# Splitting the expert weights once and keeping the halves in DRAM, in a fused filter, maxout and expert kernel

## The chip, the cores and the metric

One core of a Trainium2 chip runs the whole program. The metric is the device time of one execution in microseconds (us); three executions of the kernel before were timed. The trace is one profiled execution on that core.

## The reference, cut to what matters

Eight batches of 3072 tokens with 256 channels are filtered in the frequency domain, passed through a maxout layer and a projection, and then each token goes to one of eight experts.

```python
y = irfft(rfft(x, axis=1) * F)                      # 24576 tokens x 256
x = max(y @ w1, y @ w2, y @ w3) @ w_out             # 256 -> 768 -> 256
expert_idx = argmax(normalized(x) @ normalized(emb).T / tau)
for e in range(8):
    h = maximum(x[mask] @ w1[e], 0)                 # 256 -> 1024
    out[mask] = gate_w[mask, None] * (h @ w2[e])    # 1024 -> 256
```

With the reference's own data the experts get 6555, 2627, 10962, 295, 744, 233, 3084 and 76 tokens.

## The kernel before, in words

Every product that matters is made from operands in two parts: the high part is the operand rounded to the short type of TensorE's fast float32 (float32r), the low part is what is left, and a product is three matmuls (high by high, high by low, low by high). `split` (L189) makes the two parts of a tile: ScalarE copies the tile into the high part (L190) and VectorE subtracts (L191).

The program is written out by hand in one order (`manual_schedule`); a main loop `for x in range(18 * 49)` (L1129) walks through points. A unit `u` of 18 points carries 512 tokens through the maxout: at each point TensorE does six matmuls of 512 columns (`f_group`, L481), at points 3 to 6 the projection of the unit before (`x2_tile`, L510), at 6, 7, 11 and 12 the transform back of the unit after (`g_mm`, L451), whose data `g_load` (L431) fetches from the DRAM tensor `s2` on SyncE's queue at point 0 into tiles `gt`; `g_split` splits them at points 3 and 8. `x2_store` (L588) writes a unit's rows to the DRAM tensor `x2d`, from which tokens are gathered later. From unit 38 on (`RELEASE`, L42) the spectral stages are over and their SBUF is free.

Then the tokens go through the experts in slots: a slot is 256 tokens of one expert, and there are exactly 100 here (26, 11, 43, 2, 3, 1, 13 and 1 for the eight experts, from the counts above). The slots are listed expert by expert; `tables` (L870) turns counts into that list, for the first 12 slots early and for the other 88 at the end of the routing. `slots` (L1064) issues a slot in four steps j:

- `up(s, j)` (L1025): 12 matmuls of 256 columns, a quarter of w1 by the slot's tokens; the sum `psh` becomes `h` in two parts (ScalarE L1035, VectorE L1036).
- `down(s - 1, 0)` and `down(s - 1, 1)` (L1040) at j = 1 and 2: 24 matmuls each of the slot before by its w2; ScalarE scales the sum into `o` (L1052), and `o_store` (L1054) scatters it with two indirect DMAs from GpSimd.
- `x_load` (L985) gathers the tokens of slot s + 3 (two indirect DMAs from GpSimd), `x_turn` (L998) transposes them by DMA from SyncE's queue into `xw`, and `x_split` (L1003) joins and splits them into `xT`.
- `w_load(s + 3)` (L974): two indirect DMAs from GpSimd gather 1 MB of w1 and 1 MB of w2 of the slot's expert, as float32, into one of two buffers `raws`. Where the slot two before had the same expert, the row numbers are out of bounds and nothing is moved (L935, L940 to L944).
- `w_part(s + 1, j)` (L1014): at every j a quarter of the next slot's weights is split, whether it was loaded anew or not, into one of two buffers `ws`: one of its own (`w0`, in the trace `w`) and the memory of the maxout weights (`wt`).

So per slot TensorE has 96 matmuls of 256 columns, ScalarE and VectorE have four splits of 128 x 1024 beside their other work, and GpSimd has six indirect DMAs. The tiles `o`, `xw` and `xf` share a pool `g` of three buffers.

Of the kernel before, what the change touches and what calls it, by code (L numbers as in the profile page):

```python
# [10 lines left out]
F32 = mybir.dt.float32  # L11
F32R = mybir.dt.float32r
# [29 lines left out]
RELEASE = 18 * 38  # L42


# [66 lines left out]

def _bits(w):
    w = np.ascontiguousarray(w)
    return w.view(np.int64) if w.dtype == np.float64 else w


def _layout(inputs):
# [17 lines left out]
    c32[:, 26:26 + 128] = np.arange(128)  # L135
    return {
# [21 lines left out]
def fft_filter_maxout_moe_kernel(ctx: ExitStack, tc: tile.TileContext, I, out):  # L158
# [13 lines left out]
    lst = nc.dram_tensor("lst", (LROWS + 1, SLOT), I32, kind="Internal").ap()  # L172
    lst1 = lst.rearrange("r (c o) -> (r c) o", o=1)
# [9 lines left out]
    pidx, sgn, iotas = c32[:, 24:25], c32[:, 25:26], c32[:, 26:26 + 128]  # L183
    base_fin = const.tile([128, E], F32, name="base_fin")
# [8 lines left out]
    def body():  # L193
        st = ExitStack()
        with st:
# [231 lines left out]
            # ------------------------------------------------ back to tokens, channel major  # L427
# [48 lines left out]
            # ------------------------------------------------ maxout, projection, routing  # L476
# [33 lines left out]
            def x2_tile(u, t):  # L510
# [15 lines left out]
                def evac():  # L526
                    # lower and upper halves of the words apart, for the transposes of the slots
# [29 lines left out]
            def route2(u):  # L557
                """Steps from the norms to the one-hot choice and the gate."""
# [36 lines left out]
            def route3(u):  # L595
                """Steps from the choice to the places in the experts' lists."""
# [46 lines left out]
            # ------------------------------------------------ setup  # L643
# [21 lines left out]
            def w_split(key, n, hi, lo, late=False):  # L665
# [4 lines left out]
                # a float64 is (1 + h * 2^-20 + l * 2^-52) times a signed power of two: the high  # L670
                # part takes the first 12 bits, the low part the value of all the others
# [77 lines left out]
            class Decode:  # L749
                """Loads and decodings in order, a load ahead of the decodings, at most so many of these at a time."""  # L750
# [93 lines left out]
            def due(x):  # L844
                """Work wanted by point x: the least steep way to keep every deadline."""
# [24 lines left out]
            def tables(at, n, upto, rnd):  # L870
                """Steps to the expert and the list row of slots at .. at + n, from the counts upto."""
                tag = f"_{at}"
                cnt, ni, nf, se, ss = t8("cnt" + tag), t8("ni" + tag, dt=I32), t8("nf" + tag), t8("se" + tag), t8("ss" + tag)
# [16 lines left out]
                # list row of the slot numbered by the partition  # L890
# [8 lines left out]
                dve.tensor_scalar(out=sm, in0=pidx, scalar1=lastv, scalar2=None, op0=ALU.min)  # L899
# [164 lines left out]
            def slots(first, end):  # L1064
                """Points of the expert slots first .. end, of which lead() has made two ready."""
                for s in range(first, end + 1):
                    on, near = s < end, first < s < end - 1
                    for j in range(4):
# [9 lines left out]
                        if near:  # L1078
                            w_part(s + 1, j)
# [149 lines left out]
```

## Time and profile before

| | |
|---|---|
| median of three runs | 3392.07 us (3390.06 to 3402.77) |
| span of the profiled execution | 3398.8 us (it has no other time of its own) |
| TensorE busy | 3210.7 us, 94% |
| VectorE, ScalarE, GpSimd busy | 2499.9, 2068.2, 1541.9 us |
| DMA, mean over the span | 100 GB/s |
| first product of the slots | at 2126.8 us |
| last matmul | at 3388.1 us |

The span is the time from the first to the last instruction of the profiled execution, 6.7 us above the median of the timed runs. A TensorE that counts as busy need not run at its peak: a matmul's own time covers its way through the array, and the next begins well before it ends. How fast a row of matmuls really goes is read from the distance of their starts.

### The profile page before, as it was taken

The numbers are of one execution on the slowest core, as the hardware profiler recorded it, in microseconds if no ns is written. First come the engines' busy times: TensorE is split into PE (matmuls) and PEld (weight loads), VectorE is DVE, ScalarE is ACT, GpSimd is POOL, SyncE is SP. The second block draws the span as 40 slices with busy tenths as digits, with TensorE's granted clock in tenths as the row PEclk, the third lists the DMA queues.
The fourth block names the chain that finished last, engine by engine and source line by source line (L and its number), as shares of the span: only waits on it lengthen the run. The fifth ranks groups of instructions, "written<-read, shape, count | busy, mean of one in ns | idle before, by whom it ended". The sixth has DMA issues, their size and how long they took to land. (4 is left out here: it accounts for less than half of the span.)

```text
span 3398.8 us, 57541 instructions
## 1 busy us (share of the span) xinstructions
PE 3210.7 (94%) x20524; PEld 2860.8 (84%) x20524; DVE 2499.9 (74%) x4617; ACT 2068.2 (61%) x3818; POOL 1541.9 (45%) x1294
## 2 busy tenths in 40 slices
PE   5899999989999999999999999899999999999998
PEld 2678888878788888888888888899999999999898
DVE  7678687776788656878545555788888888888786
ACT  3444545546555554455444344788888888888786
POOL 3233233232333212333222232677777777777674
PEclk6899999999999999999999999999999999999999
DMA  8756456466554433453100120322334222224622
GB/s 247 223 135 135 126 136 142 125 120 164 122 117 112 101 122 84 98 104 94 49 26 32 32 86 23 61 65 65 107 72 113 63 65 66 66 65 127 167 65 66
DMA packets 313606, 338.58 MB, mean 100 GB/s; under 512 B 164248, under 2 KB 233251, under 8 KB 309604
## 3 DMA queue, kind: packets, MB, share of 16 engines
q1 hardware_dynamic: 217012, 197.53, 26.0%
q0 software_dynamic: 55088, 86.98, 9.5%
q10 hardware_dynamic: 41216, 50.35, 4.6%
q8 instruction: 164, 2.69, 0.4%
q14 instruction: 126, 1.03, 0.1%
HBM read 387.18 MB, written 107.42 MB: 146 GB/s over the span
## 5 line engine op out<-in xcount | busy, mean ns | idle before, releaser
L187 PE MATMUL p<-y,wt 128*128 128x512 f32 x5184 | 1327.0, 400 | 4.9 <-DVE m L498 2.9
L187 PEld LDWEIGHTS p<-y,wt 128*128 128x128 f32 x5184 | 956.9, 190 | 210.9 <-DVE m L498 3.3
L187 PEld LDWEIGHTS pso<-wo,h 128*128 128x128 f32 x3456 | 447.3, 188 | 17.5 <-DVE h L228 0.2
L187 PE MATMUL pso<-wo,h 128*128 128x264 f32 x3456 | 453.1, 285 | 0.0
L354 POOL TENSOR_TENSOR t<-t,ft 96x256 f32<-96x256 f32 (+1 forms) x176 | 178.4, 1014 | 586.7 <-DVE t L350 287.3
L191 DVE TENSOR_TENSOR wt<-r,wt 128x1024 fp32r<-128x1024 f32 x200 | 340.4, 1702 | 77.2 <-issue 53.1
L191 DVE TENSOR_TENSOR w<-r,w 128x1024 fp32r<-128x1024 f32 x200 | 336.7, 1684 | 71.9 <-issue 51.2
L1057 POOL DMA_INDIRECT out<-o,ti x200 | 286.4, 1432 | 220.0 <-ACT o L1052 186.9
L472 POOL TENSOR_TENSOR y<-df,sm 128x256 fp32r<-128x256 f32 x192 | 152.5, 795 | 501.4 <-DVE df L471 500.4
L625 POOL DMA_INDIRECT lst<-ids,pi x192 | 214.8, 1119 | 332.3 <-DVE gs L228 146.3
L187 PE MATMUL psh<-xT,wt 128*128 128x256 f32 x2400 | 322.2, 284 | 44.6 <-DVE wt L191 41.5
L977 POOL DMA_INDIRECT r<-in_e,wi x200 | 332.1, 1661 | 61.7 <-issue 31.7
L187 PE MATMUL psh<-xT,w 128*128 128x256 f32 x2400 | 325.5, 285 | 29.2 <-DVE w L191 27.4
L187 PEld LDWEIGHTS psh<-xT,wt 128*128 128x128 f32 x2400 | 297.2, 190 | 55.8 <-DVE wt L191 51.8
L190 ACT ACTIVATE wt<-r 128x1024 fp32r<-128x1024 f32 x200 | 335.9, 1680 | 0.0
L187 PEld LDWEIGHTS psh<-xT,w 128*128 128x128 f32 x2400 | 301.5, 191 | 39.6 <-DVE w L191 36.7
L190 ACT ACTIVATE w<-r 128x1024 fp32r<-128x1024 f32 x200 | 325.8, 1630 | 0.0
L227 ACT ACTIVATE h<-m 128x512 fp32r<-128x512 f32 x288 | 181.4, 630 | 236.5 <-DVE m L502 227.6
L989 POOL DMA_INDIRECT xg<-x2d,ti x200 | 285.7, 1428 | 61.9 <-issue 61.6
L187 PE MATMUL pso<-w,h 128*128 128x256 f32 x2400 | 305.6, 284 | 0.0
L187 PE MATMUL pso<-wt,h 128*128 128x256 f32 x2400 | 299.5, 280 | 4.0 <-DVE h L1036 3.4
L187 PEld LDWEIGHTS pso<-w,h 128*128 128x128 f32 x2400 | 296.3, 193 | 0.0
(159 smaller groups left out, 4809.7 us busy)
## 6 DMA issues: line engine op xcount, KB each, us to landing
ft<-in_filt SPq DMA_DIRECT2D x160, 192.0 KB
x2d<-r SPq DMA_DIRECT2D x48, 514.0 KB
xt<-in_x SPq DMA_DIRECT2D x96, 256.0 KB
s<-ot ACTq DMA_DIRECT2D x96, 256.0 KB
gt<-s SPq DMA_DIRECT2D x94, 256.0 KB
bt<-bmd SPq DMA_DIRECT2D x160, 144.0 KB
zt<-s SPq DMA_DIRECT2D x80, 192.0 KB
s<-ot ACTq DMA_DIRECT2D x80, 192.0 KB
```

Source lines behind the costliest of these rows:

```text
L187: pe.matmul(out=o, lhsT=l, rhs=r, start=start, stop=stop)
L190: act.activation(out=hi, in_=src, func=ACTF.Copy)
L191: (eng or dve).tensor_tensor(out=lo, in0=src, in1=hi.bitcast(F32), op=ALU.subtract)
L227: act.activation(out=hi, in_=src, func=ACTF.Copy)
L354: later(1, lambda: pool.tensor_tensor(out=t, in0=t, in1=fb, op=ALU.mult))
L472: later(1, lambda: pool.tensor_tensor(out=yl, in0=df, in1=sm, op=ALU.add))
L625: s = pool.indirect_dma_start(out=lst1, out_offset=bass.IndirectOffsetOnAxis(ap=pi[:, t:t + 1], axis=0), in_=ids[:, t:t + 1], in_offset=No ...
L977: pool.indirect_dma_start(out=t, out_offset=None, in_=src, in_offset=off, bounds_check=E * 128 - 1, oob_is_err=False)
L989: pool.indirect_dma_start(out=g[:, t], out_offset=None, in_=x2d[0:n], in_offset=bass.IndirectOffsetOnAxis(ap=slot[s][:, t], axis=0), bound ...
L1057: d = pool.indirect_dma_start(out=out, out_offset=bass.IndirectOffsetOnAxis(ap=slot[s][:, t], axis=0), in_=o[:, t], in_offset=None, bounds ...
```

## The change

The weights of all experts are split once, into two DRAM tensors `wsd` (16.8 MB each; a row holds the high and then the low part). `presplit` does this between units 38 and 45: 32 pieces of 128 x 1024, one every four points, each loaded on SyncE's queue (512 KB), split by ScalarE and VectorE into a tile `wsp`, and stored on SyncE's queue (1 MB). The slots then gather the two parts directly, w1 and w2 as one indirect DMA each of 2 MB (128 rows of 16 KB), into three buffers instead of two; `w_part`, `raws` and the splits in the slots are gone. A slot keeps the weights of the slot three before it, and the slot list is dealt out as three runs that take turns (`_runs`): slots 0, 3, 6, ... walk through the first third of the list, 1, 4, 7, ... through the second, and so on. The tile `o` moves from pool `g` to pool `m1`.

```diff
+NW = 3
+W_READY = RELEASE + 4 * 32 + 14
+def _runs(n):
+    at = np.arange(128)
+    size = (n + NW - 1 - np.arange(NW)) // NW
+    start = np.cumsum(size) - size
+    return np.where(at < n, start[at % NW] + at // NW, at)
...
+    wsd = [nc.dram_tensor(f"wsd_{i}", (E * 128, 4096), F32, kind="Internal").ap() for i in range(2)]
...
-                dve.tensor_scalar(out=sm, in0=pidx, scalar1=lastv, scalar2=None, op0=ALU.min)
+                dve.tensor_scalar(out=sm, in0=turn, scalar1=lastv, scalar2=None, op0=ALU.min)
...
-                    dve.tensor_tensor(out=sf, in0=es, in1=cols["es"][:, at - 2:at + n - 2], op=ALU.is_equal)
+                    dve.tensor_tensor(out=sf, in0=es, in1=cols["es"][:, at - NW:at + n - NW], op=ALU.is_equal)
...
-            def w_load(s):
-                off = bass.IndirectOffsetOnAxis(ap=cols["wi"][:, s:s + 1], axis=0)
-                for t, src in zip(raws[s % 2], (e1, e2)):
-                    pool.indirect_dma_start(
-                        out=t, out_offset=None, in_=src, in_offset=off, bounds_check=E * 128 - 1, oob_is_err=False
-                    )
+            def w_load(s, i):
+                pool.indirect_dma_start(
+                    out=ws[s % NW][i].bitcast(F32), out_offset=None, in_=wsd[i],
+                    in_offset=bass.IndirectOffsetOnAxis(ap=cols["wi"][:, s:s + 1], axis=0),
+                    bounds_check=E * 128 - 1, oob_is_err=False,
+                )
+            def presplit():
+                def load(i):
+                    e, j = divmod(i, 4)
+                    raw = raw_p.tile([128, 1024], F32, tag="raw", name="raw")
+                    src = (e1, e2)[j // 2][128 * e:128 * e + 128, 1024 * (j % 2):1024 * (j % 2) + 1024]
+                    sp.dma_start(out=raw, in_=src)
+                    return raw
+                def put(i, t):
+                    e, j = divmod(i, 4)
+                    dst = wsd[j // 2][128 * e:128 * e + 128].rearrange("p (a q) -> p a q", a=2)
+                    sp.dma_start(out=dst[:, :, 1024 * (j % 2):1024 * (j % 2) + 1024], in_=t.bitcast(F32))
+                nxt, last = load(0), None
+                for i in range(4 * E):
+                    raw, nxt = nxt, load(i + 1) if i + 1 < 4 * E else None
+                    yield
+                    t = sp_p.tile([128, 2, 1024], F32R, tag="sp", name="wsp")
+                    src = raw.rearrange("p (m c) -> p c m", c=8) if i % 4 < 2 else raw
+                    hi, lo = (t[:, a].rearrange("p (c m) -> p c m", c=8) if i % 4 < 2 else t[:, a] for a in range(2))
+                    act.activation(out=hi, in_=src, func=ACTF.Copy)
+                    yield
+                    dve.tensor_tensor(out=lo, in0=src, in1=hi.bitcast(F32), op=ALU.subtract)
+                    yield
+                    if last is not None:
+                        put(i - 1, last)
+                    last = t
+                    yield
+                put(4 * E - 1, last)
...
-                        g_p.tile([128, 2, D], F32, tag="g", name="o"),
+                        m1_p.tile([128, 2, D], F32, tag="m1", name="o"),
...
+                    if s == first:
+                        w_load(s + 2, 0)
...
-                        if near:
-                            w_part(s + 1, j)
                         if j == 2:
...
-                        if j == 3 and first < s < end - 3:
-                            w_load(s + 3)
+                            if s + 2 < end:
+                                w_load(s + 2, 1)
+                        if j == 3 and s + 3 < end:
+                            w_load(s + 3, 0)
```

A yield of `presplit` is one point. `w_first(0)` (at `W_READY`, unit 45, point 16) gathers the weights of slots 0 and 1; the third buffer is the memory of the maxout weights again, so slot 2's gather is issued at the start of slot 0.

**The order on VectorE, one slot.** Ahead of the change (`r` raw weights, `w` and `wt` the two buffers of split weights, `psh` the up product, `h` its low part, `gate`, `xf`, `xT` gates and tokens of the next slot):

```order
L191 TENSOR_TENSOR wt<-r_1_20840,wt 128x1024
L1036 SCALAR_TENSOR_TENSOR h_27694<-psh,h_27694 128x512
L1006 COPY gate<-xg 128x4
L1010 COPY xf<-xw 128x2x2x128
L191 TENSOR_TENSOR xT<-xf,xT 128x512
L191 TENSOR_TENSOR wt<-r_1_20840,wt 128x1024
L1036 SCALAR_TENSOR_TENSOR h_27747<-psh,h_27747 128x512
L191 TENSOR_TENSOR wt<-r_1_20841,wt 128x1024
L1036 SCALAR_TENSOR_TENSOR h_27806<-psh,h_27806 128x512
L191 TENSOR_TENSOR wt<-r_1_20841,wt 128x1024
L1036 SCALAR_TENSOR_TENSOR h_27830<-psh,h_27830 128x512
```

With the change:

```order
L1052 COPY gate<-xg 128x4
L1056 COPY xf<-xw 128x2x2x128
L205 TENSOR_TENSOR xT<-xf,xT 128x512
L1078 SCALAR_TENSOR_TENSOR h_28515<-psh,h_28515 128x512
L1078 SCALAR_TENSOR_TENSOR h_28575<-psh,h_28575 128x512
L1078 SCALAR_TENSOR_TENSOR h_28594<-psh,h_28594 128x512
L1078 SCALAR_TENSOR_TENSOR h_28610<-psh,h_28610 128x512
```

The four subtractions of 128 x 1024 are gone from the slot; the rest stands in the same order. ScalarE loses its four copies in the same way.

**The order on SyncE's queue, units 39 to 41.** Ahead of the change (`gt` the next unit's data, `r` a unit's finished rows):

```order
L439 DMA gt_21979<-s2_6 128x512
L593 DMA x2d<-r_22033 128x2056
L439 DMA gt_22355<-s2_6 128x512
L439 DMA gt_22357<-s2_6 128x512
L593 DMA x2d<-r_22411 128x2056
L439 DMA gt_22733<-s2_6 128x512
```

With the change (`raw` a quarter of an expert's w1 or w2, `wsp` its two parts):

```order
L607 DMA x2d<-r_21715 128x2056
L453 DMA gt_22060<-s2_6 128x512
L453 DMA gt_22062<-s2_6 128x512
L1008 DMA wsd_0<-wsp_21978 256x1x1024
L1002 DMA raw_22092<-in_e2 128x1024
L1008 DMA wsd_0<-wsp_22045 256x1x1024
L1002 DMA raw_22220<-in_e1 128x1024
L1008 DMA wsd_1<-wsp_22108 256x1x1024
L1002 DMA raw_22328<-in_e1 128x1024
L1008 DMA wsd_1<-wsp_22261 256x1x1024
L1002 DMA raw_22405<-in_e2 128x1024
L1008 DMA wsd_0<-wsp_22344 256x1x1024
```

Between two pairs of `gt` there are now four or five loads of 512 KB and as many stores of 1 MB.

**The order on GpSimd, one slot.** Ahead of the change (`out` the scatter, `xg` the token gather, `r1`, `r2` the raw weights):

```order
L1057 DMA out_0<-o_27081,ti_12_25656 24576x256 x2
L989 DMA xg_27170<-x2d,ti_12_25656 128x514 x2
L977 DMA r1_1_20840<-in_e1,wi_23147 128x2048
L977 DMA r2_1_20841<-in_e2,wi_23147 128x2048
L1057 DMA out_0<-o_27235,ti_12_25656 24576x256 x2
```

With the change (`w0`, `w1`, `wt` the three buffers; `wsd_0` holds w1, `wsd_1` w2):

```order
L1099 DMA out_0<-o_27299,ti_12_25802 24576x256 x2
L1035 DMA xg_27384<-x2d,ti_12_25802 128x514 x2
L990 DMA wt_130<-wsd_1,wi_23309 128x4096
L990 DMA w0_20835<-wsd_0,wi_23309 128x4096
L1099 DMA out_0<-o_27445,ti_12_25802 24576x256 x2
```

The count of gathers is the same. The two weight gathers of a slot now belong to different slots: w2 for the one two ahead, w1 for the one three ahead, each straight into the buffer that TensorE has just finished reading.

## Rows read from the trace of the kernel before

**Rows 1.** The head of the page: the span of the profiled execution.
```profile
span 3398.8 us, 57541 instructions
```

**Rows 2.** The view of waits, TensorE alone, 2200 to 3370 us.
```profile
PE psh L187 <- DVE wt L191: 38.4, 47, 1.6
PE psh L187 <- DVE w L191: 27.4, 46, 1.6
```

**Rows 3.** Timeline of TensorE, two slots: start us, us, what, [idle before].
```profile
2609.53 0.76 PE L187 MATMUL psh<-xT,w 128*128 128x256 f32 x5
2610.80 2.53 PE L187 MATMUL psh<-xT,w 128*128 128x256 f32 x19 [0.51 <-DVE w L191]
2613.18 2.99 PE L187 MATMUL pso<-wt,h 128*128 128x256 f32 x24
2616.01 1.60 PE L187 MATMUL psh<-xT,w 128*128 128x256 f32 x12
2617.45 2.99 PE L187 MATMUL pso<-wt,h 128*128 128x256 f32 x24
...
2621.72 0.75 PE L187 MATMUL psh<-xT,wt 128*128 128x256 f32 x5
2623.23 2.44 PE L187 MATMUL psh<-xT,wt 128*128 128x256 f32 x19 [0.76 <-DVE wt L191]
```

**Rows 4.** Timeline of TensorE, unit 46 and the first slots: slot 1 begins at 2141.63.
```profile
2090.82 2.05 PE L187 MATMUL p<-y,wt 128*128 128x512 f32 x6 [2.86 <-DVE m L498]
...
2141.63 0.75 PE L187 MATMUL psh<-xT,wt 128*128 128x256 f32 x5
...
2151.94 0.20 PE L187 MATMUL psr<-ob,tri 128*128 128x32 bf16 x2 [2.17 <-DVE ob L579]
...
2192.50 0.74 PE L187 MATMUL pso<-wt,h 128*128 128x256 f32 x4 [3.42 <-DVE h L1036]
```

**Rows 5.** Timeline of TensorE, end: slot 99 begins at 3369.01.
```profile
3369.01 0.75 PE L187 MATMUL psh<-xT,wt 128*128 128x256 f32 x5
```

**Rows 6.** The costliest groups (part 5 of the page): splits of expert weights into one buffer.
```profile
L191 DVE TENSOR_TENSOR wt<-r,wt 128x1024 fp32r<-128x1024 f32 x200 | 340.4, 1702 | 77.2 <-issue 53.1
...
L190 ACT ACTIVATE wt<-r 128x1024 fp32r<-128x1024 f32 x200 | 335.9, 1680 | 0.0
```

**Rows 7.** Windows: stretch, length, busy us of five engines, PEclk, DMA share, GB/s.
```profile
1200.00:1500.00 300.00, 299.56 (x1604) 252.61 (x1604) 214.61 (x472) 151.85 (x370) 88.60 (x91) 1.00 0.41 106
1812.00:1848.00 36.00, 36.00 (x200) 30.89 (x199) 18.71 (x47) 14.68 (x39) 8.31 (x10) 1.00 0.09 30
800.00:808.00 8.00, 8.00 (x38) 6.26 (x37) 6.69 (x15) 5.53 (x12) 0.00 (x0) 1.00 0.97 316
2580.00:2640.00 60.00, 56.78 (x469) 55.77 (x468) 49.00 (x56) 51.21 (x59) 44.31 (x30) 1.00 0.47 132
2640.00:2700.00 60.00, 56.48 (x468) 55.46 (x467) 48.89 (x54) 50.41 (x59) 44.55 (x29) 1.00 0.29 65
```

**Rows 8.** Timeline of ScalarE where it waits for a load of s2.
```profile
2022.74 0.63 ACT L227 ACTIVATE gs<-gt 128x512 fp32r<-128x512 f32 x1 [4.28 <-DMA gt<-s]
```

**Rows 9.** Timeline of GpSimd, its six gathers and scatters of one slot.
```profile
2609.67 1.91 POOL L1057 DMA_INDIRECT out<-o,ti  x1 [1.56 <-ACT o L1052]
2611.89 1.51 POOL L989 DMA_INDIRECT xg<-x2d,ti  x1 [0.30 <-issue]
2613.70 1.39 POOL L989 DMA_INDIRECT xg<-x2d,ti  x1 [0.31 <-issue]
2615.40 2.40 POOL L977 DMA_INDIRECT r<-in_e,wi  x1 [0.30 <-issue]
2618.11 0.99 POOL L977 DMA_INDIRECT r<-in_e,wi  x1 [0.30 <-DVE xf L1010]
2619.41 1.03 POOL L1057 DMA_INDIRECT out<-o,ti  x1 [0.30 <-issue]
```

**Rows 10.** Timeline of VectorE under the fourth transfer of rows 9.
```profile
2614.73 2.25 DVE L191 TENSOR_TENSOR wt<-r,wt 128x1024 fp32r<-128x1024 f32 x1
```

More of the change, by code (lines that the diff above doesn't have):

```diff
@@ L135, in _layout @@
     c32[:, 26:26 + 128] = np.arange(128)
+    c32[:, 154] = _runs(EARLY)
+    c32[:, 155] = _runs(SURE - EARLY)
     return {
@@ L183, in fft_filter_maxout_moe_kernel @@
     pidx, sgn, iotas = c32[:, 24:25], c32[:, 25:26], c32[:, 26:26 + 128]
+    runs = c32[:, 154:155], c32[:, 155:156]
     base_fin = const.tile([128, E], F32, name="base_fin")
@@ L872, in tables @@
                 tag = f"_{at}"
+                turn = runs[1 if at else 0]
                 cnt, ni, nf, se, ss = t8("cnt" + tag), t8("ni" + tag, dt=I32), t8("nf" + tag), t8("se" + tag), t8("ss" + tag)
@@ L904, in tables @@
                 dve.tensor_reduce(out=st0, in_=sel, axis=AX.X, op=ALU.add)
-                dve.tensor_tensor(out=row, in0=pidx, in1=st0, op=ALU.subtract)
+                dve.tensor_tensor(out=row, in0=turn, in1=st0, op=ALU.subtract)
                 dg = k_p.tile([128, 128], BF16, tag="lidf", name="dg")
@@ L908, in tables @@
                 dve.tensor_scalar(out=eid, in0=eid, scalar1=float(CAP // SLOT), scalar2=row, op0=ALU.mult, op1=ALU.add)
-                dve.tensor_tensor(out=row, in0=pidx, in1=lastv, op=ALU.is_gt)
+                dve.tensor_tensor(out=row, in0=turn, in1=lastv, op=ALU.is_gt)
                 dve.tensor_scalar(out=row, in0=row, scalar1=float(LROWS), scalar2=eid, op0=ALU.mult, op1=ALU.add)
@@ L1040, in down @@
             def down(s, t):
-                w, g = ws[s % 2][1], gates[s]
+                w, g = parts(s, 1), gates[s]
                 if t == 0:
                     ot[s] = (
-                        g_p.tile([128, 2, D], F32, tag="g", name="o"),
+                        m1_p.tile([128, 2, D], F32, tag="m1", name="o"),
                         pf.tile([128, 2, D], F32, tag="pf", name="pso3"),
@@ L1086, in slots, with w_first, x_first @@
                                 x_load(s + 3)
-                        if j == 3 and first < s < end - 3:
-                            w_load(s + 3)
+                            if s + 2 < end:
+                                w_load(s + 2, 1)
+                        if j == 3 and s + 3 < end:
+                            w_load(s + 3, 0)
                         yield
-            def ahead(first):
+            def w_first(first):
+                for i in range(4):
+                    w_load(first + i // 2, i % 2)
+                    yield
+            def x_first(first):
                 for i in range(3):
-                    if i < 2:
-                        w_load(first + i)
-                        yield
                     x_load(first + i)
@@ L1106, in lead @@
                 yield
-                for j in range(4):
-                    w_part(s, j)
-                    yield
-                if s + 2 < NSLOT:
-                    w_load(s + 2)
             def early():
@@ L1116, in early @@
                 yield
-                yield from ahead(0)
+                yield from x_first(0)
             sl = slots(0, SURE)
@@ L1200, in body @@
             with tc.If(nc.values_load(cols["more"], min_val=-NSLOT, max_val=NSLOT) > 0):
-                for g in (ahead(SURE), lead(SURE), lead(SURE + 1)):
+                for g in (w_first(SURE), x_first(SURE), lead(SURE), lead(SURE + 1)):
                     for _ in g:
```

47 lines of the change are left out of this document (22 added, 25 removed).

## Prediction

> **What bounds the kernel now.** I read the head of the page first: 3398.8 us from the first to the last instruction [rows 1]. The change touches two stretches, units 38 to 46 and the slots, so I asked of each which wait ends last. In the slots the view of waits names almost one thing for TensorE: the up product stands until VectorE has written the low part of the weights, 47 waits of 38.4 us for buffer `wt` and 46 of 27.4 us for `w`, about one a slot [rows 2]. The timeline shows the place. A slot begins with five matmuls that need only high parts, then a hole: 2609.53, then 2610.80; next slot 2621.72, then 2623.23 [rows 3]. Behind the hole TensorE runs without a gap: 24 matmuls from 2613.18 to 2616.01 (2.83 us), 12 from there to 2617.45 (1.44 us). A slot is four groups of 12 and two of 24, so without holes it would take 4 x 1.44 + 2 x 2.83 = **11.42 us**. What it does take: slot 1 begins at 2141.63 [rows 4], slot 99 at 3369.01 [rows 5], so 98 slots take 1227.4 us, **12.52 us** each. TensorE's own work is 98 x 11.42 = 1119.2 us, and **108 us** are holes. The 65.8 us of waits are less than that, because a matmul counts as busy until it is through the array: the first hole of rows 3 is 0.51 us of idle time, but 1.27 us from start to start with 5 x 0.12 = 0.60 us of work in it, 0.67 us lost. At 0.16 us more for each of 93 holes that is 15 us; holes of 2.17 and 3.42 us in the first slots [rows 4] add 5.6; the other 21 us have no row of their own here.
>
> **What it removes.** Each slot loses four subtractions on VectorE and four copies on ScalarE; those into `wt` alone take 340.4 and 335.9 us, 200 of 1.70 and 1.68 us [rows 6], those into `w` about as much. The holes have no other cause: the low part stands behind `xf`, `xT` and `h` on an engine that works in order. In the window from 2580 to 2640 us, 4.8 slots, VectorE is busy 49.00 us [rows 7]; less 4.8 x 4 x 1.70 = 32.6 that leaves 16.4, 27%, and ScalarE likewise 51.21 - 32.3 = 18.9, 32%. So neither is near to being the next bound, and nothing in the slot's product waits for weights that were not on chip two slots earlier. I take the whole 108 us as gain except the holes of 2.17 and 3.42 us in the first slots, whose causes (the routing of the last unit, the tables) stay. The last slot loses its hole too, about 1 us. So 108 - 6 + 1 = **-103 us**. The ends: nothing kept, -113 us, with the wait of 2.86 us in unit 46 [rows 4], where the splits of slot 0 stand; the 21 us without a row kept, -82 us.
>
> **What it adds ahead of the slots.** 32 pieces, one every four points. A unit has 108 + 72 + 24 = 204 matmuls, and the window of 36 us from 1812 shows 200 [rows 7] (a few records can be missing), so a unit is 36 us, a point 2.0 us, and a piece has 8.0 us; the pieces take seven of the ten units before the slots. ScalarE and VectorE get 4.5 pieces a unit, at 1.68 and 1.70 us: VectorE goes from 18.71 to 26.4 of 36 us, ScalarE from 14.68 to 22.3 [rows 7]. That VectorE at 73% leaves TensorE alone is in the window 1200 to 1500: 214.61 of 300 us (72%), TensorE 299.56 [rows 7]. SyncE's queue gets 0.52 MB in and 1.05 MB out every 8.0 us, 197 GB/s, on top of the 30 GB/s of those units: 227 GB/s for 256 us. The nearest rows for what the transfers can carry: 316 GB/s at a share of 0.97, for the 8 us from 800 [rows 7]; and 106 GB/s at 0.41, which would be 259 at a full share. So the load is 70 to 88% of it. What is queued behind: each unit's `gt` comes after up to one store and one load. Where `gt` came late before, behind a burst of gathers, ScalarE stood 4.28 us [rows 8], and TensorE, which has five sums ahead of it, showed no hole there. Seven units at that price on the path would be 30 us, at none 0; I take **+2 us**, nearer the row in which TensorE did not notice.
>
> **What it adds in the slots.** From the expert counts: the first 12 slots are all of expert 0 and load once for each of three buffers; of the other 88 the runs are 30, 29 and 29 long, the second is expert 2 throughout, the first changes twice, the third five times, and two begin with a new expert. That makes 3 + 2 + 2 + 5 = 12 loads of 4.2 MB, where 14 of 2.1 MB were. Each comes as two gathers of 2.1 MB most of a slot apart, with two slots (22.8 us) to land, 92 GB/s. A window with two loads of 2.1 MB in it shows 132 instead of 65 GB/s, and TensorE's busy time is 56.78 against 56.48 us [rows 7]: they cost nothing. Two loads stand back to back once, slots 13 and 14. I take **+3 us**, from 0 to 12 (one hole of 1 us for each load). The third buffer holds the maxout weights until unit 47 ends; slot 2 needs it two slots later, 22.8 us, the same time as any other. That `o` has buffers of its own lets the transposes start earlier; it hides behind TensorE and counts nothing.
>
> **The sum.** -103 + 2 + 3 = -98 us against the span, 3398.8 to 3300.8. The median of the runs is 6.7 us below that span, so I forecast **3294 us**. Its own range is 3279 (-113) to 3315 (-82 and the 5 us of costs).
>
> **GpSimd, and one rule.** It issues six transfers a slot: 1.91, 1.51, 1.39, 2.40, 0.99 and 1.03 us, 9.23 in all, with 0.30 us ahead of each 11.03 us, the rest of 12.5 being a wait for `o` [rows 9]. That fits into 11.42, with 0.4 us to spare. The long ones share a cause: the transfer issued at 2615.40 began under a subtraction that ran from 2614.73 for 2.25 us [rows 10] and ended 0.82 us after it, while the one at 2618.11 took 0.99. The Trainium skill says in "SBUF — State Buffer", section "Who interferes with whom", that a VectorE instruction with two SBUF inputs contends with a GpSimd one that reads SBUF. By that rule the six would take about 1.0 us each, 7.8 us a slot with their gaps; by the durations as they are 11.03; the sum is the same by both, since both are under 11.42, but the first makes the rival below less likely. The same passage infers that a plain tensor-tensor subtraction should not hold up the writing of descriptors, with which this row does not agree.
>
> **Rival 1: GpSimd paces the slots.** The new gathers name rows of 16 KB where rows of 8 KB were named. If both of a slot took 2.40 us, the cycle would be 11.03 + 1.4 = 12.4 us and nothing would be won; at half that, 11.7 us, the loss is 0.3 x 98 = 30 us; I take 12.0 us, 57 us lost, **3351 us**. It decides above 11.42 us. For it: 0.4 us to spare. Against it: the row at 0.99 us, and the subtractions that go. With it I count transposes or gathers made late by bursts and `gt` late at its full 30 us, 3315 to 3362. Chance 0.14.
>
> **Rival 2: the queue of SyncE overruns, and it gets slower.** ScalarE works in order; if a piece is not there, it stands, and TensorE with it five sums later. 50.3 MB in the 256 us of the plan, plus the 98 us won, is the point from which it decides: 50.3 / 354 = 142 GB/s, with 30 beside it 172 GB/s in all. At 160 the pieces get 130 GB/s and take 387 us, 131 us too long: 3294 + 131 = **3425 us**. For it: no stretch of the trace holds more than 200 GB/s for 256 us [rows 7], and loads and stores share one queue. Against it: 316 GB/s where the share was full, and larger packets here. Chance 0.07, of which 0.02 in mild forms that stay faster.
>
> **Rival 3: the slots keep their pace.** Were the holes only the last of several waits that end together, 12.5 us a slot would stay: 3392 us, unchanged. Against it: the five high-part matmuls start on time with tokens and buffers at hand [rows 3]. Chance 0.05.
>
> **Rival 4: the change does not do what it says**, the flag for the kept weights fails, and every slot moves 4.2 MB: with 316 - 65 = 251 GB/s for them 16.7 us a slot, 98 x 4.2 = 410 us more, 3802 us. The flag compares with the slot three before, as the deal needs; chance 0.04.
>
> **How the numbers follow.** Forecast 0.70, rivals 0.14, 0.05, 0.07, 0.04 (in the order 1, 3, 2, 4). A measurement of this kernel tells 0.5% (17 us) from no change. Faster: 0.70 + 0.14 + 0.02 = 0.86; same: 0.05; slower: 0.05 + 0.04 = 0.09. The range 3279 to 3340 holds the forecast and most of rival 1's nearer forms, 0.80.
>
> **What would show it.** Right: slots 11.4 us apart; no waits of the up product for VectorE; GpSimd's transfers near 1.0 us; in units 38 to 45 VectorE near 73%, some 225 GB/s, TensorE still at full. Wrong: TensorE waiting there for ScalarE while ScalarE waits for `raw` or `gt`; waits for the weight gathers at slots 13, 14 or 54 to 59; GpSimd without idle time.

## The result, and the profile after

The changed kernel takes **3318.1 us** (median of four runs, 3312.0 to 3319.0) where the kernel before took 3391.2 us beside it: a ratio of 0.9772, 95% interval 0.9749 to 0.9794, 73 us faster. The forecast was 3294 us, 24 us less; the range (3279 to 3340) holds the time, the forecast's own part of it (3279 to 3315) does not. The profiled execution is the fastest of the four (3312.0 us, span 3310.1).

The slots first. In the timeline of TensorE the holes of [rows 3] are gone; a slot starts at 2609.82 and the next at 2621.24, 11.42 us later (start us, us, what, how many matmuls):

```profile
2609.82 2.99 PE L201 MATMUL psh<-xT,wt 128*128 128x256 f32 x24
2612.65 3.04 PE L201 MATMUL pso<-w,h 128*128 128x256 f32 x24
2615.53 1.58 PE L201 MATMUL psh<-xT,wt 128*128 128x256 f32 x12
2616.95 3.04 PE L201 MATMUL pso<-w,h 128*128 128x256 f32 x24
2619.82 1.58 PE L201 MATMUL psh<-xT,wt 128*128 128x256 f32 x12
2621.24 3.04 PE L201 MATMUL psh<-xT,w 128*128 128x256 f32 x24
```

What TensorE waits for is no longer VectorE [rows 2] but the tokens (`xT`). The view of waits, from 1700 us to the end (us in total, times, longest):

```profile
PE psh L201 <- ACT xT L204: 17.4, 3, 10.8
PE pso L201 <- ACT m L508: 2.6, 1, 2.6
PE p L201 <- DVE m L512: 1.0, 1, 1.0
```

GpSimd's transfers, which took 0.99 to 2.40 us [rows 9], take 1.0 us each (groups of GpSimd from 2320 to 2740 us: count, busy us, mean ns, idle before):

```profile
L1035 POOL DMA_INDIRECT xg<-x2d,ti x74 | 76.5, 1033 | 22.6 <-issue 22.3 <-DMA wt<-wsd,wi 0.3
L1099 POOL DMA_INDIRECT out<-o,ti x73 | 73.7, 1010 | 152.7 <-ACT o L1094 147.6 <-ACT h L1077 4.8 <-issue 0.3
L990 POOL DMA_INDIRECT w<-wsd,wi x48 | 47.9, 997 | 14.6 <-issue 14.6
L990 POOL DMA_INDIRECT wt<-wsd,wi x25 | 24.9, 997 | 7.6 <-issue 7.6
```

In the units that carry the splitting TensorE runs through until 1956 us. In the two windows shown VectorE is busy 24.5 to 25.5 of 36 us, ScalarE 21, and the DMA engines move 238 to 245 GB/s (windows of a unit's length, columns as in [rows 7]); the three windows behind them have 214 to 238 GB/s, and VectorE at up to 25.9 us:

```profile
1776.00:1812.00 36.00, 36.00 (x200) 30.89 (x199) 25.54 (x52) 21.26 (x45) 8.37 (x11) 1.00 0.84 245
1812.00:1848.00 36.00, 36.00 (x200) 30.89 (x199) 24.51 (x51) 21.12 (x44) 8.95 (x11) 1.00 0.83 238
```

So all that the prediction wanted to see in the steady parts is there. What is left is at the loads: starts of two matmuls lie 11.1 us apart at 2287 (ahead of slot 14) and 4.4 us at 2770 (ahead of slot 55). TensorE stood in both, and behind each is a stretch at a granted clock of 0.50, the lower of its two levels.

### The profile page after: what moved, and what is told of

Its sections match the earlier page's. It is cut to its first block, busy times and chain, and to the rows that moved or that the text cites. A ratio compares the mean times of both kernels' runs of the same rounds, so it can differ in the third digit from the quotient of the medians.

```text
span 3310.1 us, 56666 instructions
## 1 busy us (share of the span) xinstructions
PE 3186.3 (96%) x20524; PEld 2858.4 (86%) x20524; DVE 1916.9 (58%) x4249; ACT 1527.8 (46%) x3450; POOL 1245.5 (38%) x1294
## 4 chain that ended last, share of the span: by engine, by line
PE 55%; issue 19%; POOL 13%; DMA 7%; DVE 4%; ACT 1%; POOLq 1%; SPq 0%; ACTq 0%; DVEq 0%
PE p L201 32%; PE pso L201 13%; POOL out L1099 4%; POOL xg L1035 4%; POOL w L990 4%; PE psi L201 2%; PE psb L201 2%; DMA bt<-bmd 2%; PE psy L201 2%; PE psa L201 2%; POOL wt L990 2%; DMA ft<-in_filt 1%; DMA xw<-xg 1%; DMA s<-ot 1%; PE psh L201 1%
## 5 line engine op out<-in xcount | busy, mean ns | idle before, releaser
L1078 DVE SCALAR_TENSOR_TENSOR h<-psh,h 128x512 fp32r<-128x512 f32 x400 | 275.4, 689 | 459.6 <-ACT h L1077 458.0
L201 PE MATMUL psh<-xT,w 128*128 128x256 f32 x3216 | 418.0, 285 | 7.0 <-ACT xT L204 6.6
L201 PEld LDWEIGHTS psh<-xT,w 128*128 128x128 f32 x3216 | 401.8, 193 | 8.0 <-ACT xT L204 7.0
L201 PE MATMUL pso<-w,h 128*128 128x256 f32 x3216 | 407.9, 283 | 0.6 <-ACT o L1094 0.6
L201 PEld LDWEIGHTS pso<-w,h 128*128 128x128 f32 x3216 | 395.7, 192 | 0.8 <-ACT o L1094 0.8
L1077 ACT ACTIVATE h<-psh 128x512 fp32r<-128x512 f32 x400 | 237.1, 593 | 268.6 <-PE psh L201 268.6
L1094 ACT ACTIVATE o<-pso,gate 128x256 f32<-128x256 f32 x200 | 94.8, 474 | 423.3 <-PE pso L201 416.5
L516 DVE TENSOR_TENSOR m<-p,m 128x512 f32<-128x512 f32 x288 | 197.4, 686 | 93.7 <-PE p L201 91.0
L242 DVE TENSOR_TENSOR h<-m,h 128x512 fp32r<-128x512 f32 x288 | 210.0, 729 | 67.1 <-ACT h L241 66.2
L512 DVE TENSOR_TENSOR m<-p,m 128x512 f32<-128x512 f32 x288 | 197.0, 684 | 75.7 <-PE p L201 73.4
L542 ACT COPY r<-pso 128x512 uint16<-128x512 uint16 x192 | 112.5, 586 | 262.9 <-PE pso L201 262.9
```

The lines of the kernel that those rows point to most:

```text
L201: pe.matmul(out=o, lhsT=l, rhs=r, start=start, stop=stop)
L242: later(1, lambda: dve.tensor_tensor(out=lo, in0=src, in1=hi.bitcast(F32), op=ALU.subtract))
L512: dve.tensor_tensor(out=m2, in0=ps, in1=m_t[u, fc], op=ALU.max)
L516: dve.tensor_tensor(out=m2, in0=ps, in1=m2, op=ALU.max)
L1077: act.activation(out=h[:, 0], in_=ps, func=ACTF.Relu)
L1078: dve.scalar_tensor_tensor(out=h[:, 1], in0=ps, scalar=0.0, in1=h[:, 0].bitcast(F32), op0=ALU.max, op1=ALU.subtract,)
```

## The experiments

Twelve kernels ran, four on each of three chips, called A, B and C here, beside runs of the kernel before. The chips differ: the kernel before took 3393.4 us on B, but 3414.6 and 3413.9 us on A and C. So times are compared on one chip only. (The expectations of after_2 and apart call the chip of the result above the first, and A the second.)

| chip | kernel | median us | ratio to before, 95% interval |
|---|---|---|---|
| A | no_loads | 3353.8 | 0.9837 (0.9815 to 0.9859) |
| A | x_ahead | 3357.7 | 0.9838 (0.9820 to 0.9857) |
| A | slots_no_split | 3362.5 | 0.9850 (0.9823 to 0.9878) |
| A | list_order | 3481.4 | 1.0214 (1.0184 to 1.0244) |
| B | after_2 | 3320.1 | 0.9786 (0.9770 to 0.9803) |
| B | no_loads_2 | 3295.7 | 0.9711 (0.9695 to 0.9728) |
| B | apart | 3296.5 | 0.9720 (0.9704 to 0.9736) |
| B | halves | 3311.8 | 0.9757 (0.9740 to 0.9773) |
| C | slots_no_split_2 | 3351.6 | 0.9812 (0.9791 to 0.9834) |
| C | presplit_fast | 3426.6 | 1.0026 (1.0011 to 1.0040) |
| C | o_in_g | 3362.5 | 0.9835 (0.9811 to 0.9858) |
| C | apart_spread | 3340.6 | 0.9785 (0.9771 to 0.9800) |

### The weight loads taken away (no_loads, no_loads_2; beside after_2, the changed kernel again)

```diff
-                    dve.tensor_tensor(out=sf, in0=es, in1=cols["es"][:, at - NW:at + n - NW], op=ALU.is_equal)
+                    dve.memset(sf, 1.0)
```

> The flag for kept weights is set for every slot after the first twelve, so no weights are gathered any more in the slots (slots of other experts are computed with wrong weights; this kernel leaves out the late weight gathers and nothing else). Theory (bursts of weight gathers starve the token transposes): the holes near slots 14, 54 to 56 and the half-clock stretches behind them go, some 20 to 26 us: 3292 to 3298 us against 3318 of the changed kernel. Rival A (the shortfall is the splitting ahead of the slots, which stays as it is here): 3315 to 3320 us. Rival B (only the holes at half clock count, the other gathers are free): about 3300 us with all holes but one gone.

> The changed kernel itself, unedited, beside the others on one chip, since the chip of the first four experiments ran the kernel before at 3415 us instead of 3391 and each slot there took 0.4 us more than 11.4. If the chip makes that difference: on a chip like the first the ratio to the kernel before is 0.977 (3318 of 3391), on one like the second some 0.985 to 0.99. If the edits made it: 0.977 on any chip, and ScalarE takes the first half of each output sum 0.3 us after its last matmul started.

> The same kernel as no_loads (late slots compute with weights of other experts; their weight gathers are left out), now beside the changed kernel on one chip. Theory (bursts of weight gathers starve the token transposes): 20 to 26 us below after_2, and no hole of 4 us or more in the slots after the first ten. Rival A (the shortfall is the splitting ahead of the slots): within 5 us of after_2.

The first run tells nothing of the loads by itself: 3353.8 us where 3292 to 3298 were expected, on a chip that shows waits of its own (below). On chip B the changed kernel again stood at 0.9786, and without late loads it takes 3295.7 us, **24.4 us less**, at the upper end of the 20 to 26 expected. The waits of TensorE in the slots, after_2 first:

```profile
PE psh L201 <- ACT xT L204: 19.6, 2, 16.2
```

and no_loads_2, where the one left is at slot 1, as in after_2:

```profile
PE psh L201 <- ACT xT L204: 2.8, 1, 2.8
```

The hole is at slot 14. The timeline of after_2 there:

```profile
2274.89 1.00 POOL L990 DMA_INDIRECT w<-wsd,wi  x1 [0.30 <-issue]
2276.18 0.99 POOL L990 DMA_INDIRECT wt<-wsd,wi  x1 [0.30 <-issue]
...
2277.00 2.80 SPq L1047 DMA_TRANSPOSE xw<-xg  x2
...
2286.28 1.00 POOL L990 DMA_INDIRECT wt<-wsd,wi  x1 [0.30 <-issue]
...
2292.87 1.60 PE L201 MATMUL psh<-xT,w 128*128 128x256 f32 x12
2309.16 0.76 ACT L1055 COPY xf<-xw 128x512 uint16<-128x512 uint16 x1 [19.94 <-DMA xw<-xg]
2310.64 1.74 PE L201 MATMUL psh<-xT,wt 128*128 128x256 f32 x4 [16.17 <-ACT xT L204]
```

SyncE issues the two transposes of slot 14's tokens from 2277.00 on, just behind two gathers of weights (2.1 MB each); a third gather follows at 2286.28. ScalarE, which copies the tokens, has stood 19.94 us when it gets them at 2309.16; TensorE has nothing else to do and stands 16.17 us. From 2282 to 2288 us the view of DMA queues (packets, MB, share of the engines' time) shows how the two share the engines, GpSimd's gathers and scatters, weights for the most part, in the first line, the transposes in the second. For each packet of the first, up to 16 KB, one of 256 bytes goes:

```profile
q0 software_dynamic: 159, 2.19, 94.8%
q1 hardware_dynamic: 161, 0.04, 3.0%
```

The windows of the whole stretch:

```profile
2280.00:2290.00 10.00, 10.00 (x86) 10.00 (x86) 2.55 (x5) 2.74 (x5) 5.55 (x6) 1.00 1.03 364
2290.00:2300.00 10.00, 4.47 (x38) 4.26 (x36) 0.00 (x0) 0.00 (x0) 0.51 (x1) 0.96 1.15 107
2300.00:2310.00 10.00, 0.00 (x0) 0.00 (x0) 0.46 (x1) 0.81 (x2) 0.00 (x0) 0.50 0.96 167
2310.00:2320.00 10.00, 9.22 (x55) 8.92 (x56) 3.81 (x7) 3.68 (x8) 5.06 (x5) 0.69 0.28 66
```

In three windows TensorE has 38 + 0 + 55 = 93 matmuls where 3 x 86 fit: 165 missing, at 8.6 a us **19.2 us**. Of the 31 missing in the last window 6 are the end of the hole (0.64 us), 25 the half clock behind it. The spans differ by 24.7 us (3315.8 and 3291.1); another 4.8 us lie ahead of the first product of the slots (2124.6 against 2119.7 us), where the two run the same work, so they are spread between executions. From the start of slot 1 to that of slot 99, which leaves them out, after_2 takes 1147.6 us, no_loads_2 1127.7 and the profile of the result 1148.1: about **20 us** are the loads' price.

### The second half of the output sum behind the fourth up group (apart)

```diff
-                        if j in (1, 2):
+                        if j in (1, 3):
...
-                                down(s - 1, j - 1)
+                                down(s - 1, j // 2)
...
-                        if j == 2:
+                        if j == 3:
                             if s > first:
                                 o_store(s - 1)
...
-                            if s + 2 < end:
-                                w_load(s + 2, 1)
-                        if j == 3 and s + 3 < end:
-                            w_load(s + 3, 0)
+                            if s + 2 < end:
+                                w_load(s + 2, 1)
+                            if s + 3 < end:
+                                w_load(s + 3, 0)
```

> The second half of the output sum of a slot is put behind the fourth up group instead of the third, with its stores and the two weight gathers. It tells whether the 0.45 us that TensorE stood in every slot of the second chip comes from its waiting for ScalarE to read the first half out of the same PSUM tile: if so that hole is gone wherever it was, and the time is some 40 us below after_2 on a chip like the second, and within 8 us of after_2 on one like the first. Rival (the late reading is a sign of something else that is late, for instance TensorE itself): the hole moves to another place and the time stays with after_2 within 8 us.

That was a miss with the better outcome: on a chip where at most 8 us were expected the time fell to 3296.5 us, 23.6 below after_2 and level with no loads at all. No hole at slot 14, the one wait left is slot 1's:

```profile
PE psh L201 <- ACT xT L204: 2.1, 1, 2.1
```

The timeline says why. The tokens' gather no longer stands behind the output's scatter, which waits for ScalarE, so GpSimd issues that of slot 14 some 8 us earlier (2261.49 where after_2 has 2273.56, of which 3.7 us are the earlier start of the slots), and SyncE the transposes behind it. Here they go out ahead of the two gathers of weights, not behind them:

```profile
2261.49 1.00 POOL L1035 DMA_INDIRECT xg<-x2d,ti  x1 [0.30 <-issue]
...
2267.82 3.78 SPq L1047 DMA_TRANSPOSE xw<-xg  x2
...
2268.94 1.04 POOL L990 DMA_INDIRECT w<-wsd,wi  x1 [0.31 <-issue]
2270.28 1.01 POOL L990 DMA_INDIRECT wt<-wsd,wi  x1 [0.31 <-issue]
...
2284.44 0.76 ACT L1055 COPY xf<-xw 128x512 uint16<-128x512 uint16 x1
```

ScalarE copies them at 2284.44 without a wait. The gathers of weights hardly move within a slot: the first of the two goes out 9.3 us ahead of the start of slot 13 here, 7.9 us in after_2. So it was the tokens that were late, not the weights. Of the kernels with the full computation on that chip, both originals among them, this is the fastest, and from slot 1 to slot 99 it takes 1127.4 us, as without loads; its interval (0.9704 to 0.9736) lies below that of the changed kernel (0.9770 to 0.9803).

### The tokens a slot earlier (x_ahead)

```diff
-                            if s + 2 < end:
-                                x_turn(s + 2)
-                            if s + 3 < end:
-                                x_load(s + 3)
+                            if s == first:
+                                x_turn(s + 2)
+                                if s + 3 < end:
+                                    x_load(s + 3)
+                            if s + 3 < end:
+                                x_turn(s + 3)
+                            if s + 4 < end:
+                                x_load(s + 4)
...
-                xw[s] = g_p.tile([128, 2, 4, 128], U16, tag="g", name="xw")
+                xw[s] = (y_p if 3 <= s < SURE else g_p).tile([128, 2, 4, 128], U16, tag="y" if 3 <= s < SURE else "g", name="xw")
```

> The tokens of a slot are gathered and transposed one slot earlier than in the changed kernel, the weights when they were. Theory (tokens starved beside weight gathers): one more slot (11.4 us) of slack covers most of the hole of 11.1 us at slot 14 and all of that of 4.4 us at slot 55: 3298 to 3306 us. Rival A (splitting ahead of the slots): 3315 to 3320. Rival B (the weights themselves land late, not the tokens): 3315 to 3320 as well, and the holes stay, with TensorE waiting for a gather of weights. Rival C: tokens queued earlier on GpSimd and SyncE collide with more of the weight packets, 3320 to 3330.

It ran on chip A, so 3357.7 us is to be held against no_loads there: 3.9 us more. The wait of the up product after 2230 us is one, half of that in after_2:

```profile
PE psh L201 <- ACT xT L204: 7.5, 1, 7.5
```

It stands ahead of slot 15, at 2343.13 us, and not ahead of slot 14: a slot more of slack moves the hole and shrinks it, and does not close it. The changed kernel did not run on this chip, so the gain itself is not measured.

### Three loads in a row (list_order)

```diff
-                turn = runs[1 if at else 0]
+                turn = pidx
```

> The changed kernel with the slots of the list taken in its own order, not dealt out to three runs: at each change of expert three slots in a row load 4.2 MB each, 12.6 MB in a burst, at six places. Theory (bursts starve the token transposes): a hole of 11 us or more at each change, slots 14's being the model, six bursts of three: 6 times 10 to 20 us, 3365 to 3430 us. Rival (what counts is the number of loads, at 2 us each): 18 or so loads instead of 12, about 3325 to 3335 us.

3481.4 us, 127.6 above no_loads on the same chip, slower than the kernel before. The waits of TensorE, and one of the windows:

```profile
PE psh L201 <- ACT xT L204: 93.8, 5, 28.7
```

```profile
2620.00:2640.00 20.00, 0.00 (x0) 0.00 (x0) 0.00 (x0) 0.00 (x0) 0.00 (x0) 0.50 0.90 168
```

So five holes where six were expected, the longest 28.7 us, the first only 3.7; the granted clock of 0.50 in and behind them takes part of the rest. After 2230 us the gathers move 16 loads of 4.2 MB here, 9 in the changed kernel; the 16 cost 110.8 us from slot 1 to slot 99 (1281.1 against 1170.3 in no_loads), the 9 about 20. So their number alone does not set the price; it rises where they follow one another. Why equal bursts leave holes of 3.7 and of 28.7 us stays open.

### Weight rows of 8 KB (halves)

```diff
-                pool.indirect_dma_start(
-                    out=ws[s % NW][i].bitcast(F32), out_offset=None, in_=wsd[i],
+                for a in range(2):
+                    pool.indirect_dma_start(
+                        out=ws[s % NW][i].bitcast(F32)[:, 2048 * a:2048 * a + 2048], out_offset=None, in_=wsd[i][a],
```

The high and the low parts have DRAM tensors of their own for that, each with its own store.

> Each gather of weights in rows of 16 KB is made two gathers in rows of 8 KB, of the same bytes. Theory (transposes in packets of 256 bytes take turns with weight packets, so their delay goes with the size of a weight packet): the transposes beside the 8.4 MB of slots 13 and 14 take about half of 24 us, the hole of 11 us shrinks to 0 to 4 us, 8 to 20 us below after_2. Rival A (the delay goes with the bytes of the burst): holes as in after_2, within 5 us. Rival B (GpSimd now issues eight transfers a slot, 8 times 1.3 us = 10.4 of 11.4 us, and paces the slots in places): slower than after_2 by 10 us or more.

8.3 us less than after_2, at the edge of what the theory gave. The one wait in the slots is still there:

```profile
PE psh L201 <- ACT xT L204: 12.0, 1, 12.0
```

That lies between the 10.8 and 16.2 us of the changed kernel's two profiles. The same six us of the view of queues, 2282 to 2288, show that the turns did what the theory says, with almost twice as many of either packet as in after_2:

```profile
q0 software_dynamic: 307, 2.25, 97.5%
q1 hardware_dynamic: 293, 0.08, 5.8%
```

Yet the hole did not halve. So turns by packet are shown, but the delay as a whole does not go with the size of a packet; what makes up the rest of it, and whether the 8.3 us are the rows' doing, stays open. Rival B fell: with eight transfers a slot GpSimd is busy 1446.5 us instead of 1245.7, and no slot is longer.

### `o` back in the shared pool (o_in_g)

```diff
-                        m1_p.tile([128, 2, D], F32, tag="m1", name="o"),
+                        g_p.tile([128, 2, D], F32, tag="g", name="o"),
```

> The changed kernel with the tile of the output rows back in the pool of three buffers that it shared in the kernel before with the transposed tokens. The prediction counted its own buffers as nothing. If the slack of the token transposes is what covers a load of weights: the holes grow, that at slot 14 by up to a slot and holes at other changes of expert appear, 5 to 40 us above the changed kernel (3325 to 3360). If it counts nothing: 3314 to 3322.

On chip C it stands at 0.9835, and the changed kernel did not run there. The trace shows one wait of the up product after 2230 us, between the longest ones of the changed kernel's two profiles, and no new hole at other loads; so nothing speaks against counting it at nothing:

```profile
PE psh L201 <- ACT xT L204: 14.5, 1, 14.5
```

### The removal by itself (slots_no_split, slots_no_split_2)

```diff
             def w_part(s, j):
+                if s >= 2:
+                    return
```

> The kernel before, with its splits of the weights left out in slots 2 and later (those slots are computed with weights of other slots; everything else stays, the loads of the raw weights too). It measures the removal alone. Theory (the splits cost 103 us and the change gives some back in its loads): 3285 to 3293 us, below the changed kernel by 25 to 33 us, no waits of the up product for VectorE. Rival (the removal was never worth more than what the changed kernel shows): 3313 to 3320 us.

> The same kernel as slots_no_split (the kernel before with no splits of weights in slots 2 and later, which are computed with weights of other slots), on another chip. It prices the removal by itself, without the work ahead of the slots. As the prediction has it (103 us): 3288 to 3291 us where the kernel before takes 3391 to 3393, and 5 to 8 us below no_loads_2 (3295.7), which carries the removal and the splitting ahead of the slots. Rival A (the splitting ahead of the slots costs its worst, 30 us): 3265 to 3270. Rival B (it costs nothing): 3294 to 3298.

They ran on chips A and C: 52 and 62 us below the kernel before, not 103. On these chips, in every kernel that ran there, a slot has a wait that chip B lacks. The timeline of no_loads, TensorE and ScalarE:

```profile
2604.63 3.04 PE L201 MATMUL pso<-w,h 128*128 128x256 f32 x24
2607.51 1.57 PE L201 MATMUL psh<-xT,wt 128*128 128x256 f32 x12
2609.27 3.14 PE L201 MATMUL pso<-w,h 128*128 128x256 f32 x24 [0.19 <-ACT o L1094]
```

```profile
2608.74 0.47 ACT L1094 ACTIVATE o<-pso,gate 128x256 f32<-128x256 f32 x1 [3.23 <-PE pso L201]
```

and the same place in the changed kernel where it was first measured:

```profile
2604.07 1.60 PE L201 MATMUL psh<-xT,w 128*128 128x256 f32 x12
2604.27 0.47 ACT L1094 ACTIVATE o<-pso,gate 128x256 f32<-128x256 f32 x1 [2.28 <-PE pso L201]
```

ScalarE takes the first half of the output sum 0.20 us after the next group begins there, but 1.23 us after it here, and the second half of the sum, in the same PSUM tile, starts only then: its wait in the third row ends with ScalarE's reading. That costs 0.23 to 0.38 us a slot in these kernels (what starts over 0.15 us apart have above 0.12, from 2420 to 2720 us). Why the signal is late on these chips stays open. It is not all: slots_no_split_2 takes 1161.7 us from slot 1 to slot 99, 34.0 more than no_loads_2 on chip B; the signal makes some 23 of them, and longer waits in slots 3 and 4 most of the rest. These chips are slower ahead of the slots too: unit 38, up to which all kernels do nearly the same work, begins at 1773.0 to 1780.8 us there, at 1757.4 to 1761.1 on B. What can be said of the removal: on chip B no_loads_2, which has the removal, the splitting ahead and the first three loads, is 97.7 us below the kernel before.

### The pieces twice as fast (presplit_fast)

```diff
                     dve.tensor_tensor(out=lo, in0=src, in1=hi.bitcast(F32), op=ALU.subtract)
-                    yield
                     if last is not None:
                         put(i - 1, last)
                     last = t
-                    yield
```

> The changed kernel with a piece of the weights split every two points (4 us) instead of every four: for 128 us the pieces ask for 393 GB/s, beside the 30 of those units. It is the dose for the rival that the queue of SyncE overruns. If ScalarE, which works in order, stands for pieces that are late: at 316 GB/s in all, of which 286 for the pieces, they take 176 us, 48 too long, so 15 to 50 us above the changed kernel (3333 to 3370), with TensorE waiting for ScalarE in units 38 to 43. If nothing waits that is not covered: 3315 to 3325.

3426.6 us, 64 above o_in_g on the same chip where 15 to 50 were expected, and level with the kernel before (1.0026). ScalarE waits for the raw pieces (waits from 1700 to 2000 us), TensorE for ScalarE and VectorE behind it; the window shows 231 matmuls in 60 us where 333 fit:

```profile
ACT wsp L1017 <- DMA raw<-in_e: 88.6, 29, 11.2
```

```profile
PE p L201 <- ACT m L508: 17.8, 7, 6.0
```

```profile
1830.00:1890.00 60.00, 45.77 (x231) 35.91 (x230) 38.63 (x69) 31.00 (x52) 9.71 (x10) 0.97 0.99 301
```

So the pieces do overrun what the transfers carry, at a share of 0.99 and 275 to 301 GB/s: four units from 1780 us on take 202.6 us instead of 144. The rival's mechanism is real, and the pace of one piece in 8 us keeps clear of it.

### The first gathers spread (apart_spread)

```diff
                     w_load(first + i // 2, i % 2)
-                    yield
+                    for _ in range(4 if first == 0 else 1):
+                        yield
```

> The kernel apart (3296.5 us) with the first four gathers of weights, 8.4 MB in unit 46, spread over 32 us instead of 8. If the burst is what makes gt late there (ScalarE stands 11.4 us for it, TensorE 2.6 us, and half clock for 3.4 us behind): the hole goes, 3 to 5 us: 3291 to 3294. Rival (the gathers now meet the tokens of slots 0 and 1, whose transposes wait instead): 3296 to 3302, with a hole of 4 us or more at slot 1.

3340.6 us on chip C. The question stays open: the burst was not spread. The first three of the four gathers are issued at 2062.67, 2064.09 and 2065.43 us all the same, only the fourth later (2094.63), `gt` is late as before, and the wait of 2.6 us in unit 46 is unchanged. What the run does show is the order of apart on a chip with the late signal: 21.9 us below o_in_g beside it, with 0.10 us a slot lost to the late signal, not 0.23.

## Why the prediction was right, and which term was mis-sized

**The slots' holes, -103 us: right.** From the first product of the slots to the last group of matmuls the kernel before takes 2126.76 to 3385.06 us, 1258.3:

```profile
2126.76 1.59 PE L187 MATMUL psh<-xT,w 128*128 128x256 f32 x12
...
3385.06 3.09 PE L187 MATMUL pso<-wt,h 128*128 128x256 f32 x24 [0.56 <-ACT o L1052]
```

no_loads_2, with the holes gone and no late loads, takes 2119.75 to 3277.42, 1157.7:

```profile
2119.75 1.59 PE L201 MATMUL psh<-xT,w 128*128 128x256 f32 x12
...
3277.42 3.13 PE L201 MATMUL pso<-w,h 128*128 128x256 f32 x24 [0.61 <-ACT o L1094]
```

That is 100.6 us less. The steady slot is 11.42 us, and neither VectorE nor ScalarE became the next bound. Rival 3 is out. The one trace of the kernel before is slower than its median, so the size may be some us too large, in the prediction as here. The forecast's end with nothing kept adds up to 112 us from its terms (108, 1 and 2.9), not 113; nothing hangs on it.

**The splitting ahead, +2 us (0 to 30): its end at nothing.** TensorE runs through in the units shown; VectorE is at 68 to 72% where 73% was worked out. From unit 38, where the splitting begins, to the first product of the slots the changed kernel takes 363.8 and 363.4 us in its two profiles, the kernel before 364.5: about 1 us less, not 2 more. That the first product comes 2 to 8 us earlier is for the most part spread ahead of unit 38, where both do nearly the same work. In unit 46 there is a wait that the prediction did not price: behind the first four gathers of weights ScalarE stands 11.8 us for `gt`, and TensorE the 2.6 us shown above. That the total still falls fits the splits of slot 0, which are gone from there. Rival 2 did not occur; the dose shows that it would have at half the spacing.

**GpSimd: it does not pace the slots, and the rule holds.** The six transfers take 6.1 us a slot, 7.9 with the 0.3 us ahead of each, as was worked out for a slot without the subtractions. So far the trace agrees with the Trainium skill's "SBUF — State Buffer", section "Who interferes with whom", that a VectorE instruction with two SBUF inputs contends with a GpSimd one that reads SBUF. The kernel before with only its splits left out (slots_no_split_2) shows the same, 996 ns for each of 52 gathers of raw weights, so it is the splits, not the new gathers. That it is their subtractions and not ScalarE's copies is in the trace of the kernel before: of 511 transfers of GpSimd that begin between 2300 and 3360 us, the 339 that begin under a subtraction of 128 x 1024 end 0.80 to 0.93 us after it, every one; the other 172 take 0.99 to 1.08 us, though 84 of them begin under such a copy. The passage's inference that a plain subtraction does not hold up the writing of descriptors is against these rows.

**The loads in the slots, +3 us (0 to 12): mis-sized, and this is the step that failed.** They cost about 20 us of TensorE's time in the traces, 19.2 of it at slot 14 in after_2, and 24.4 us by the medians of after_2 and no_loads_2. The forecast asked whether the weights have time to land, and named slots 13 and 14 as the one place with two loads back to back. It took the price from a window of the kernel before with 2.1 MB loads far apart [rows 7], and gave nothing to what is queued beside them: transposes of 256-byte packets, issued right behind 16 KB rows. Rival 1 did name it, in half a sentence and without a row: "transposes or gathers made late by bursts", 3315 to 3362 us. The time of 3318 us lies there and outside the forecast's own 3279 to 3315; the stated range holds it because it was stretched over that rival, whose main part, GpSimd's pace, did not occur. So that the range held is in part luck.

The Trainium skill says in "DMA: Bandwidth & Descriptors", section "Queues, rings and completion order", that an engine takes turns between queue rows at the granularity of packets. The trace agrees: 161 of the small packets beside 159 large ones in 6 us, and 293 beside 307 with halved rows. By that rule alone, halving the rows should have about halved the delay, and the hole does not show that.

The sum with the measured terms: -100.6 for the slots, 20 for the loads and -1 ahead of the slots, -81 to -82 us. Between the two profiles it is 3398.8 - 3310.1 = 88.7, since 7.6 us more lie ahead of unit 38; between the medians it is 73, since the profile of the changed kernel lies 6 us under its median and that of the kernel before above its own.

## What to carry to other kernels

When a change makes some transfers larger, price not only whether these land in time but also every small transfer issued behind it until the burst is through. The order of issue is then worth as much as the bytes: letting the tokens' gather and transposes go out ahead of the weights gave back all that the burst had cost, with nothing moved less. And price a hole on TensorE with the half clock that follows it.

## What the runs showed that was not expected

- Behind the stretch in which transposes and weight rows take turns, the DMA engines count as fully busy and carry little: 107 GB/s at a share of 1.15 from 2290 to 2300 us in after_2. Being in flight together is not enough for that: the ten us before have 364 at 1.03, with both under way from 2282 on. Why it drops stays open. In apart, with its order, the window at a full share that carries least has 203 GB/s:

```profile
2286.00:2296.00 10.00, 10.00 (x86) 10.00 (x85) 4.18 (x7) 3.09 (x7) 5.81 (x7) 1.00 1.01 203
```

- The same kernel differs between chips in where it waits: ScalarE hears of the first half of an output sum about 1 us later on two of the three chips of these experiments. The kernel before with its splits left out gained 52 and 62 us there, where the slots on B gave up 100.6 with the changed kernel's edits and no late loads.
